# Top-k attention with a mixture-of-depths block: the gate dot products split over GpSimd and ScalarE, all slot picks on VectorE, and the bounds' bits tested once at the end

## The chip, the cores and the metric

The kernel runs on one core of one Trainium2 chip. The metric is the device time of one execution in microseconds (us); a smaller number is better. Five engines run side by side, each through its own instructions in order: TensorE (PE; its weight loads are listed apart as PEld), VectorE (DVE), ScalarE (ACT), GpSimd (POOL) and SyncE (SP), which issues DMAs. An instruction starts when those in front of it on its engine allow it and the semaphores that it waits for have been raised.

## What is computed

For 8 batches and 8 heads, with 576 tokens of 64 dimensions, the reference keeps the 32 largest scores of each query row, takes a softmax over them and multiplies by v. The heads side by side give x (576 tokens x 512). A gate per token is the dot product of x with `w_gate`; the 128 tokens of a batch with the largest gates get an update by a two-layer network:

```python
scores = scale * np.matmul(q, k.transpose(0, 1, 3, 2))
kth = np.partition(scores, -top_k, axis=-1)[..., -top_k:-top_k + 1]
scores = np.where(scores >= kth, scores, -1000000000.0)
...
scores = np.einsum('bsd,d->bs', x, w_gate)
top_idx = np.argpartition(-scores[b], capacity)[:capacity]
ye = np.maximum(x[b, top_idx] @ w1, 0.0) @ w2
g = 1.0 / (1.0 + np.exp(-scores[b, top_idx]))
out[b, top_idx] = x[b, top_idx] + g[:, None] * ye
```

## The kernel before

**Units and steps.** The work is cut into 144 units, 18 per batch: a unit is one block of query rows (t = 0 to 3 with 128 rows each, t = 4 with the last 64) and two heads (four for t = 4). The loop at L1094 walks over steps n; in each step different units stand at different stages, so that a unit takes five steps to pass through. In step n:

- PE: `weigh` (L1036) turns the scores of unit n-4 into `ptr` and `av` in nine pairs of matmuls, and the second of each pair adds the mask `less`; then it turns 0 to 2 loaded pieces of the next batch's q and k, multiplies the scores of unit n+1 (`multiply`, L355), multiplies unit n-4's weights with v (`values`, L503), and runs what the mixture of an earlier batch has due (`h_ps`, `y_ps`, `pick`).
- ACT: two exponentials of unit n-4 out of `ptr` and `av` (outputs `pT` and `last`), half the mask of unit n-3 (`less`), copies of what PE turned (`kT`, `qT`) and of earlier mixture results, the scores of unit n+1 out of PSUM (`sc<-ps`), the values of unit n-4 (`xs<-av`), and two `sides` instructions with a sum for unit n-1. The callbacks in the list `late` run at `flush()` (L1127), behind the mask and in front of the copies.
- POOL: the other half of the mask of unit n-3, then what stands in `vector_late` and `pool_late`, then two multiplications `y<-sc,sides` of unit n-1 and a small `fill`.
- DVE: `find_bound` (L386) for unit n, in two halves with `flush_vector()` between them (L394), then `find_kth` (L437) for unit n-2.

`ptr`, `av` and the score PSUM tile have one buffer each. `keep_in_program_order` fixes every engine's order as it is written; no scheduler changes it.

**The gates.** When the last unit of a block t is through, `normalise` (L543) divides by the sums, one step later: a reciprocal on DVE and the multiplication `x<-xs,rden` on POOL, put at the front of `vector_late`. One step later again `gates` (L954) computes the dot product with `wg` on DVE in one instruction with a sum (`prod<-x,wg`, L940). Counted in steps i = 0 to 17 of a batch, `normalise` stands at i = 2, 4, 8, 12 and 16 and the gate at i = 3, 5, 9, 13 and 17; i = 5 belongs to the block of 64 rows of the batch before.

**The mixture.** `mixture` (L599) is a generator that is advanced at the steps of `mix_at` (L984). The gates go to DRAM and come back as a row on all partitions; per block t, `choose` (L637) counts on DVE how many gates are larger (`junk<-gate_row,gate`, which gives the rank) and `choose_slot` (L656) marks the slot of each rank in `pick` with a comparison: on DVE for t = 0, on POOL for the other four. PE then uses `pick` to place rows, fetched by an indirect DMA from POOL. The last batch goes through `closing` (L746), written out by hand.

**The checks.** `keep_least` (L1073) reduces, once per batch on DVE, the bounds, the values found and the bounds' low mantissa bits (`low`, an integer operation) to one column each of `least`. At the end (L1255 to L1278) nine reductions are folded into `sure`; PE sums it over partitions (`count_unsure`, L1285), and a branch at L1368 runs a general path if a count is off. In PE's order the matmul of `sure` stands behind the four transposes of `xe` of the last batch and in front of that batch's matmuls with w1 and w2.

Of the kernel before, what the change touches and what calls it, by code (L numbers as in the profile page):

```python
# [10 lines left out]
AF = mybir.ActivationFunctionType  # L11
ALU = mybir.AluOpType
FP32 = mybir.dt.float32
BF16 = mybir.dt.bfloat16
I32 = mybir.dt.int32
# [11 lines left out]
LEAST = 1.0e-16 * SMALLER  # L27
# [4 lines left out]
J = 4  # L32
# [16 lines left out]
def kernel(  # L49
# [12 lines left out]
    P = nc.NUM_PARTITIONS  # L62
    B, H, S, D = q.shape
# [5 lines left out]
    R = S - JP  # L69
# [8 lines left out]
    const = ctx.enter_context(tc.tile_pool(name="const", bufs=1))  # L78
# [4 lines left out]
    stats = ctx.enter_context(tc.tile_pool(name="stats", bufs=6))  # L83
    ptpool = ctx.enter_context(tc.tile_pool(name="pt", bufs=2))
    xpool = ctx.enter_context(tc.tile_pool(name="x", bufs=2))
    modpool = ctx.enter_context(tc.tile_pool(name="mod", bufs=1))
# [43 lines left out]

    NS = B * 2 * (J * NHP + NHP // 2)
    seen = const.tile([P, NS], FP32, name="seen")
    least = const.tile([P, 3, B], FP32, name="least")
    sums = const.tile([P, B * NT, H], FP32, name="sums")
    nc.gpsimd.memset(sums, 1.0)

# [27 lines left out]
    wg = const.tile([P, HD], FP32, name="wg")  # L164
# [3 lines left out]
    def load_weights():  # L168
# [6 lines left out]
    pe, dve, act, pool, sp = (  # L175
        InOrder(tc, e)
        for e in (nc.tensor, nc.vector, nc.scalar, nc.gpsimd, nc.sync)
    )


    late, vector_late, pool_late = [], [], []
# [5 lines left out]
    def flush():  # L187
        while late:
            late.pop(0)()
# [353 lines left out]
    def normalise(b, t, xs):  # L543
        n = R if t == J else P
        den = sums[0:n, b * NT + t, :]
        divide(n, xs, of_batch[b][0][0:n, t, :], den)
# [52 lines left out]
    def mixture(row0, pg, rank, exact=False):  # L599
# [8 lines left out]
        if exact:  # L608
            for t0, t1, at in ((0, J, 0), (J, NT, JP)):
                tr = ps_misc.tile([P, 512], FP32, name="tr", tag="misc")  # L610
                n = R if t0 else P
# [6 lines left out]
                w = (t1 - t0) * n  # L618
                act.copy(out=gate_row[:, at : at + w], in_=tr[:, 0:w])
        else:  # L620
            row_dram = drampool.tile([1, S], FP32, name="row_dram")
            sp.dma_start(
                out=row_dram[0, 0:JP].rearrange("(p j) -> p j", j=J), in_=gate[:, 0:J]
            )
            sp.dma_start(
                out=row_dram[0, JP:S].rearrange("(p j) -> p j", j=1),
# [6 lines left out]
        for t in range(NT):  # L633
            yield
            n = R if t == J else P

            def choose(t=t, n=n):  # L637
                junk = modpool.tile([P, S], FP32, name="junk", tag="scratch")
                dve.tensor_scalar(
                    out=junk[0:n, :],  # L640
                    in0=gate_row[0:n, :],
                    scalar1=gate[0:n, t : t + 1],
                    scalar2=None,
                    op0=ALU.is_gt,
                    op1=ALU.add,
                    accum_out=rank[0:n, t : t + 1],
                )
                if exact:
                    break_ties(t, gate, gate_row, rank)

                if t == 0:
                    choose_slot(dve, t, n)
                else:
                    pool_late.append(lambda: choose_slot(pool, t, n))

            def choose_slot(engine, t, n):  # L656
                engine.tensor_scalar(
                    out=pick[0:n, t, :],
                    in0=slot[0:n, :],
                    scalar1=rank[0:n, t : t + 1],  # L660
                    scalar2=None,
                    op0=ALU.is_equal,
                )

            vector_late.append(choose)
# [288 lines left out]
    def gates(b, t):  # L954
        dot_tile(t, *of_batch[b])

    def dot_tile(t, x, pg):
        n = R if t == J else P
        dot(n, x[0:n, t, :], pg[0][0:n, t : t + 1])
# [70 lines left out]
    of_batch = {}  # L1030
# [40 lines left out]
        find_kth(ys.pop(n), next8s[b][:, i, :, :])  # L1071

    def keep_least(b, bound, kth):  # L1073
        low = stats.tile([P, per_batch, 2], I32, name="low", bufs=1)
        dve.tensor_scalar(
            out=low,
            in0=bound.bitcast(I32),
            scalar1=(1 << 23) - 1,
            scalar2=1,
            op0=ALU.bitwise_and,  # L1080
            op1=ALU.bitwise_xor,
        )
        for w, of in enumerate((bound, kth, low)):
            dve.tensor_reduce(
                out=least[:, w, b : b + 1], in_=of, axis=mybir.AxisListType.XY, op=ALU.min
            )

    def mask_of(n, on=None):
        b, i = divmod(n, per_batch)
# [4 lines left out]
    for n in range(-1, N):  # L1094
        b, i = divmod(n, per_batch)
        if i == 0 and 0 <= b < B - 1:
            qkv[b + 1] = room_for_qkv(b + 1)
            loading = chain(
                loading, Rows(k[b + 1], q[b + 1], *qkv[b + 1][0:2]).parts()
            )  # L1100
        if 0 < n + 1 < NHP:
            turn_pair(first_rows, n + 1)
        if n == 1:
            load_v(v[0], qkv[0][2])
        if n == NHP:
            load_weights()


        gating = normalised
        if inverting is not None:  # L1110
            normalised = inverting[0:2]
            vector_late.insert(0, lambda a=inverting: normalise(*a))
            inverting = None
        else:
            normalised = None
        if gating is not None:
            vector_late.append(lambda a=gating: gates(*a))

        if is_unit(n - 4):
            tr, av = room_to_turn()
            pT, last, exp = weigh(scs.pop(n - 4), tr, av, masks.pop(n - 4))
            exp()
        if is_unit(n - 3):
            mask_of(n - 3, (act, None) if n in scatter_steps else None)
        flush()  # L1127
        if is_unit(n + 1):
            b, t, g = units[n + 1]
            ps = room_for_scores()  # L1130
            kT, qT = qkv[b][0:2]
            b, i = divmod(n, per_batch)
            loads = list(islice(loading, first_loads[i] if b == 0 else loads_at[i]))
            halves = [ps[:, a, :, HALF : HALF + P] for a in range(2)]
            for load, half in zip(loads, halves):
                load[0](half)
            multiply(t, g, kT, qT, ps)
            for load, half in zip(loads, halves):
                load[1](half)
            scs[n + 1] = keep(ps, n == -1)  # L1140
        if is_unit(n - 4):
            b4, t4, g4 = units[n - 4]
            values(t4, g4, pT, last, av, qkv[b4][2])
            if n in place_steps:
                values_bank[0] = av
                next(mixtures[place_steps[n]])
            if g4 == 0:
                xs = xpool.tile([P, H, DE], FP32, name="xs")
                if t4 == 0:
                    x = xpool.tile([P, NT, HD], FP32, name="x")  # L1150
                    pg = gates_of[b4 % 2]
                    of_batch[b4] = x, pg
            keep_values(t4, g4, av, xs)
            if g4 == groups(t4) - 1:
                inverting = b4, t4, xs
                n4 = R if t4 == J else P
                keep_sums(n4, xs, sums[0:n4, b4 * NT + t4, :])
            while kept:
                kept.pop(0)()


        if is_unit(n):
            bound_of(n)
        flush_vector()
        flush_pool()
        if is_unit(n - 2):
            kth_of(n - 2)
        while after_kth:
            after_kth.pop(0)()


        if is_unit(n - 1):
            what_is_below(n - 1)

        if gating is not None:
            b, t = gating
            if t == J:
                store(out[b], of_batch[b][0])
                mixtures[b] = mixture(float(b * S), of_batch[b][1], ranks[:, b, :])
        for b in mix_steps.get(n, ()):  # L1180
            next(mixtures[b], None)
        b, i = divmod(n, per_batch)
        if i == v_at and 0 <= b < B - 1:
            load_v(v[b + 1], qkv[b + 1][2])
# [68 lines left out]


    keep_least(B - 1, bounds.pop(B - 1)[:, :, :, 7], next8s.pop(B - 1)[:, :, :, 7])  # L1255
    sure = stats.tile([P, 1], FP32, name="sure")
    dve.memset(sure, 1.0)
    for what, op, than, limit in (
        (least[:, 0, :], ALU.min, ALU.is_gt, LEAST),
        (least[:, 1, :], ALU.min, ALU.is_gt, LEAST),  # L1260
        (least[:, 2, :], ALU.min, ALU.is_gt, 0.5),
        (seen, ALU.max, ALU.is_lt, float(MIDDLE)),
        (seen, ALU.min, ALU.is_gt, float(MIDDLE - 16)),
        (sums.rearrange("p t h -> p (t h)"), ALU.min, ALU.is_gt, FEWEST),
        (sums.rearrange("p t h -> p (t h)"), ALU.max, ALU.is_lt, MOST),
    ):
        far = stats.tile([P, 1], FP32, name="far")
        dve.tensor_reduce(out=far, in_=what, axis=mybir.AxisListType.X, op=op)
        dve.scalar_tensor_tensor(
            out=sure, in0=far, scalar=limit, in1=sure, op0=than, op1=ALU.mult  # L1270
        )
# [133 lines left out]
```

## Time and profile before

| what | value |
|---|---|
| time, median of 3 runs | 825.23 us (824.99 to 825.73) |
| profiled execution | 828.44 us; span of its instructions 826.1 us |
| mean granted TensorE clock | 0.99 |
| DVE busy | 787.2 us, 95% of the span |
| PE busy; weight loads | 777.0 us, 94%; 596.5 us, 72% |
| ACT busy | 730.7 us, 88% |
| POOL busy | 715.4 us, 87% |

The profile is of one execution. "Busy" is time in which an engine ran instructions; overlapping instructions count once, so a group's number of instructions times its mean duration can be more than its busy time. A row of the instruction timeline gives the start, the time taken, engine, line, operation, output<-inputs, shapes and the number of instructions merged; behind it, in brackets, idle time of the engine just before and what ended it. L45 is the line of a helper through which all instructions go, so that they are told apart by their tiles. The distance from one start to the next on a busy engine is what an instruction really costs there, and it is shorter than its duration where the next one starts inside it. The list of waits gives engine, tile, what was waited for, total us, times and the longest.

### The profile page before, as it was taken

Reading aid. Unit: us, or ns where it says so; the run is one execution under the profiler, and the core shown is the slowest. Engines: PE = TensorE matmul, PEld = TensorE weight load, DVE = VectorE, ACT = ScalarE, POOL = GpSimd, SP = SyncE. Lnnn points to the kernel's source line nnn. Section 1 sums busy time; section 2 is a strip of 40 time slices with the busy share of each in tenths; the row PEclk is TensorE's granted clock in tenths of the full one; section 3 lists DMA queues with packets and bytes.
Section 4 is the critical chain, followed back from the end, with each engine's and each line's share of the span. In section 5 each row is a group of like instructions: output and inputs, shape, how many; then the busy total and the mean of one; then the engine's idle time right before and its main releaser. Section 6 shows DMA issues by size and latency. Waiting matters only on the chain. (4 is left out here: it accounts for less than half of the span.)

```text
span 826.1 us, 28252 instructions
## 1 busy us (share of the span) xinstructions
PE 777.0 (94%) x10143; PEld 596.5 (72%) x10143; DVE 787.2 (95%) x4651; ACT 730.7 (88%) x1557; POOL 715.4 (87%) x722
## 2 busy tenths in 40 slices
PE   6888888888999999999999999999999999999976
PEld 5566666666887778877787777877787777767744
DVE  7899999999999999999999999999999999999960
ACT  4799999999999999999999999999999999879831
POOL 3799999999899999999899999999999998899831
PEclk9699999999999999999999999999999999999999
DMA  7931111521141221521223221512215102101021
GB/s 170 283 86 40 28 66 28 105 53 27 60 92 36 53 40 59 112 47 34 79 47 86 53 40 60 104 23 54 40 59 112 28 15 66 23 12 18 2 71 30
DMA packets 122133, 50.38 MB, mean 61 GB/s; under 512 B 116417, under 2 KB 116417, under 8 KB 120961
## 3 DMA queue, kind: packets, MB, share of 16 engines
q1 hardware_dynamic: 118672, 43.91, 22.0%
q0 software_dynamic: 1728, 4.20, 2.8%
q8 instruction: 82, 1.34, 0.8%
q14 instruction: 67, 0.54, 0.3%
q10 hardware_dynamic: 1584, 0.39, 0.2%
HBM read 36.93 MB, written 11.55 MB: 59 GB/s over the span
## 5 line engine op out<-in xcount | busy, mean ns | idle before, releaser
L45 POOL TENSOR_TENSOR y<-sc,sides 128x576 f32<-128x576 f32 x288 | 365.1, 1289 | 57.0 <-ACT sides L45 54.3
L45 DVE MAX8 cand<-sc 128x8 f32<-128x82 f32 (+1 forms) x2016 | 314.0, 228 | 2.7 <-ACT sc L45 2.7
L45 POOL TENSOR_SCALAR less<-sc,next 128x576 bf16<-128x576 f32 x135 | 232.5, 1722 | 12.9 <-DVE next L45 10.0
L45 PE MATMUL ptr<-out_of_reach,less 128*128 128x128 bf16 x1136 | 205.3, 220 | 19.5 <-POOL less L45 19.4
L45 ACT ACTIVATE sides<-sc,bound 128x576 bf16<-128x576 f32 x288 | 223.0, 787 | 0.0
L45 PE MATMUL ptr<-ident,sc 128*128 128x128 f32 x1136 | 217.0, 282 | 0.0
L45 DVE MAX8 next<-y 128x8 f32<-128x584 f32 x288 | 204.4, 751 | 1.7 <-POOL y L45 1.6
L45 PEld LDWEIGHTS av<-v,pT 128*64 128x64 f32 x4544 | 144.1, 137 | 66.9 <-ACT last L45 63.2
L45 PE MATMUL ps<-kT,qT 64*128 64x288 f32 (+1 forms) x1280 | 182.0, 431 | 5.2 <-ACT qT L45 5.2
L45 PEld LDWEIGHTS ptr<-ident,sc 128*128 128x128 f32 x1136 | 161.3, 142 | 29.1 <-issue 17.4
L45 ACT ACTIVATE pT<-ptr 128x1024 f32<-128x1024 f32 x142 | 145.3, 1023 | 33.2 <-PE ptr L45 32.2
L45 PE MATMUL av<-v,pT 128*64 128x65 f32 x4544 | 163.7, 224 | 9.3 <-ACT last L45 8.5
L45 ACT COPY sc<-ps 128x1152 f32<-128x1152 f32 (+1 forms) x144 | 162.2, 1126 | 3.5 <-PE ps L45 3.5
L45 PEld LDWEIGHTS <-less 128*128 128x128 bf16 x1296 | 136.1, 106 | 39.2 <-POOL less L45 25.2
L45 PEld LDWEIGHTS ps<-kT,qT 64*128 64x128 f32 (+1 forms) x1280 | 100.2, 178 | 41.5 <-issue 21.2
L45 ACT ACTIVATE less<-sc,next 128x576 bf16<-128x576 f32 x143 | 111.2, 777 | 12.7 <-DVE next L45 10.8
L45 DVE MATCH_REPLACE8 cand<-best,cand 128x21 f32<-128x21 f32 (+1 forms) x576 | 99.0, 180 | 0.0
L45 DVE MAX8 best<-cand 128x8 f32<-128x21 f32 (+1 forms) x576 | 90.5, 190 | 0.0
L45 PE MATMUL h_ps<-xeT,w 128*128 128x128 f32 x464 | 65.8, 286 | 0.0
L45 PEld LDWEIGHTS h_ps<-xeT,w 128*128 128x128 f32 x464 | 55.8, 191 | 9.2 <-issue 5.8
L45 PE MATMUL y_ps<-w,hT 128*128 128x512 f32 x112 | 60.6, 636 | 0.0
L45 ACT ACTIVATION_READ_ACCUMULATOR sides<-sc,bound 128x1 f32 x288 | 59.9, 208 | 0.0
(133 smaller groups left out, 866.4 us busy)
## 6 DMA issues: line engine op xcount, KB each, us to landing
v<-in_v_dram SPq DMA_DIRECT2D x64, 128.0 KB, 4.2
out_dram<-x SPq DMA_DIRECT2D x8, 1024.0 KB, 3.9
rows<-in_k_dram SPq DMA_DIRECT2D x56, 128.0 KB, 2.9
rows<-in_q_dram SPq DMA_DIRECT2D x56, 128.0 KB, 3.1
w<-in_moe_w_dram SPq DMA_DIRECT2D x2, 2048.0 KB
gate_row<-row_dram SPq DMA_DIRECT2D x7, 288.0 KB, 4.4
w<-in_k_dram SPq DMA_DIRECT2D x8, 128.0 KB, 3.2
last<-in_k_dram SPq DMA_DIRECT2D x8, 128.0 KB, 4.0
```

The source lines that it names most:

```text
L45: return lambda *a, **kw: self._tc.keep_in_program_order(fn(*a, **kw))
```

## The change

The dot product becomes two instructions. Right behind the division, POOL multiplies x by `wg` into `xs` (`weigh_gates`); in the next step ACT copies `xs` onto itself with a sum into the gate (`sum_gates`), from the list `late`. DVE no longer computes the gates of the steps in the loop (38 of the 40 blocks); the last two blocks of the last batch still use the old `gates` on DVE. All five slot picks of a batch go to DVE, each with a sum into an unused column `some` (`accum_out`), one step behind their ranks; in `closing` the picks are as they were. Per batch, the integer operation and two of the three reductions of `keep_least` go; instead ACT copies the 36 bounds of each partition into `bounded`. Behind the loop the last copy is issued by a `flush()`, and then one integer operation on 288 columns and reductions over 288 columns instead of 8 do the tests.

In the built program the order of PE's and of SP's instructions is the same as before.

```diff
-    least = const.tile([P, 3, B], FP32, name="least")
+    least = const.tile([P, B], FP32, name="least")
+    bounded = const.tile([P, NS], FP32, name="bounded")
...
-                if t == 0:
-                    choose_slot(dve, t, n)
-                else:
-                    pool_late.append(lambda: choose_slot(pool, t, n))
-
-            def choose_slot(engine, t, n):
-                engine.tensor_scalar(
+                if t:
+                    choose_slot(t - 1)
+                if t == J:
+                    choose_slot(t)
+
+            def choose_slot(t):
+                n = R if t == J else P
+                some = stats.tile([P, 1], FP32, name="some")
+                dve.tensor_scalar(
                     out=pick[0:n, t, :],
                     in0=slot[0:n, :],
                     scalar1=rank[0:n, t : t + 1],
                     scalar2=None,
                     op0=ALU.is_equal,
+                    op1=ALU.add,
+                    accum_out=some[0:n, :],
                 )
...
+    def weigh_gates(b, t, xs):
+        n = R if t == J else P
+        pool.tensor_tensor(
+            xs[0:n, :, 0:D],
+            of_batch[b][0][0:n, t, :].rearrange("p (h d) -> p h d", h=H),
+            wg[0:n, :].rearrange("p (h d) -> p h d", h=H),
+            ALU.mult,
+        )
+
+    def sum_gates(b, t, xs):
+        n = R if t == J else P
+        act.activation(
+            xs[0:n, :, 0:D],
+            xs[0:n, :, 0:D],
+            AF.Copy,
+            accum_out=of_batch[b][1][0][0:n, t : t + 1],
+        )
...
     def keep_least(b, bound, kth):
-        low = stats.tile([P, per_batch, 2], I32, name="low", bufs=1)
-        dve.tensor_scalar(
-            out=low,
...
-        for w, of in enumerate((bound, kth, low)):
-            dve.tensor_reduce(
-                out=least[:, w, b : b + 1], in_=of, axis=mybir.AxisListType.XY, op=ALU.min
-            )
+        at = 2 * per_batch * b
+        late.append(
+            lambda: act.copy(
+                out=bounded[:, at : at + 2 * per_batch].rearrange("p (n i) -> p n i", i=2),
+                in_=bound,
+            )
+        )
+        dve.tensor_reduce(
+            out=least[:, b : b + 1], in_=kth, axis=mybir.AxisListType.XY, op=ALU.min
+        )
...
-            normalised = inverting[0:2]
-            vector_late.insert(0, lambda a=inverting: normalise(*a))
+            normalised = inverting
+
+            def divide_and_weigh(a=inverting):
+                normalise(*a)
+                weigh_gates(*a)
+
+            vector_late.insert(0, divide_and_weigh)
...
         if gating is not None:
-            vector_late.append(lambda a=gating: gates(*a))
+            late.append(lambda a=gating: sum_gates(*a))
...
     keep_least(B - 1, bounds.pop(B - 1)[:, :, :, 7], next8s.pop(B - 1)[:, :, :, 7])
+    flush()
+    low = modpool.tile([P, S], I32, name="low", tag="scratch")[:, 0:NS]
+    dve.tensor_scalar(
+        out=low,
+        in0=bounded.bitcast(I32),
...
-        (least[:, 0, :], ALU.min, ALU.is_gt, LEAST),
-        (least[:, 1, :], ALU.min, ALU.is_gt, LEAST),
-        (least[:, 2, :], ALU.min, ALU.is_gt, 0.5),
+        (bounded, ALU.min, ALU.is_gt, LEAST),
+        (least, ALU.min, ALU.is_gt, LEAST),
+        (low, ALU.min, ALU.is_gt, 0.5),
```

More of the change, by code (lines that the diff above doesn't have):

```diff
@@ L1073, in keep_least @@
     def keep_least(b, bound, kth):
-        low = stats.tile([P, per_batch, 2], I32, name="low", bufs=1)
-        dve.tensor_scalar(
-            out=low,
[L1077 to L1081, printed above, removed]
-        )
-        for w, of in enumerate((bound, kth, low)):
-            dve.tensor_reduce(
-                out=least[:, w, b : b + 1], in_=of, axis=mybir.AxisListType.XY, op=ALU.min
-            )
+        at = 2 * per_batch * b
[4 more added lines that the diff above has]
+            )
+        )
+        dve.tensor_reduce(
+            out=least[:, b : b + 1], in_=kth, axis=mybir.AxisListType.XY, op=ALU.min
+        )
     def mask_of(n, on=None):
@@ L1175 @@
         if gating is not None:
-            b, t = gating
+            b, t, _ = gating
             if t == J:
@@ L1255 @@
     keep_least(B - 1, bounds.pop(B - 1)[:, :, :, 7], next8s.pop(B - 1)[:, :, :, 7])
+    flush()
[3 more added lines that the diff above has]
+        in0=bounded.bitcast(I32),
+        scalar1=(1 << 23) - 1,
+        scalar2=1,
+        op0=ALU.bitwise_and,
+        op1=ALU.bitwise_xor,
+    )
     sure = stats.tile([P, 1], FP32, name="sure")
```

## The prediction, made before the changed kernel ran

> **What bounds the kernel now.** I read the busy times stage by stage first. The columns are the stretch, its length, then busy time of PE, PEld, DVE, ACT and POOL, the granted clock, DMA share and GB/s; the rows are batch 1, batch 4 and batch 7 (the last).
>
> ```profile
> 102.90:197.90 95.00, 83.34 (x1187) 63.31 (x1188) 94.93 (x563) 88.60 (x190) 88.51 (x88) 1.00 0.25 55
> ...
> 390.30:486.40 96.10, 94.93 (x1263) 73.59 (x1262) 95.99 (x578) 91.51 (x196) 88.52 (x88) 1.00 0.27 60
> ...
> 678.60:778.70 100.10, 96.92 (x1273) 75.82 (x1271) 98.03 (x589) 87.25 (x183) 89.84 (x89) 1.00 0.13 28
> ```
>
> DVE is never idle in batches 1 to 6. In batch 1 it is alone; in batch 4, which is like 2, 3, 5 and 6, PE is as full, and ACT lacks 4.6 us. Being full does not make DVE the bound, so I looked at whom the others wait for, in batches 3 to 5:
>
> ```profile
> ACT pT L45 <- PE ptr L45: 11.9, 33, 0.6
> ...
> POOL less L45 <- DVE next L45: 3.9, 10, 0.6
> ```
>
> ACT's idle time is waiting for PE's turned scores, 4.0 us per batch; waits for DVE are 1.3 us per batch, on POOL. The timeline of ACT's exponentials shows how. Counting from step i = 0 of batch 4:
>
> ```profile
> 395.97 1.03 ACT L45 ACTIVATE pT<-ptr 128x1024 f32<-128x1024 f32 x1
> ...
> 401.23 1.00 ACT L45 ACTIVATE pT<-ptr 128x1024 f32<-128x1024 f32 x1
> ...
> 406.53 1.02 ACT L45 ACTIVATE pT<-ptr 128x1024 f32<-128x1024 f32 x1
> ...
> 422.55 1.02 ACT L45 ACTIVATE pT<-ptr 128x1024 f32<-128x1024 f32 x1 [0.51 <-PE ptr L45]
> ...
> 443.89 1.02 ACT L45 ACTIVATE pT<-ptr 128x1024 f32<-128x1024 f32 x1 [0.51 <-PE ptr L45]
> ```
>
> From 390.67 (i = 0) to 412.07 (i = 4) ACT hardly stops: its own work sets these steps, 5.3 us each. From i = 4 to 17 it waits for PE in nearly each step. There PE has no gap; one step of it:
>
> ```profile
> 426.31 0.27 PE L45 MATMUL ptr<-ident,sc 128*128 128x128 f32 x1
> ...
> 427.85 0.39 PE L45 MATMUL ps<-ident,rows 128*128 128x128 f32 x2
> 428.17 1.24 PE L45 MATMUL ps<-kT,qT 64*128 64x288 f32 x8
> 429.34 1.15 PE L45 MATMUL av<-v,pT 128*64 128x65 f32 x32
> 430.33 0.39 PE L45 MATMUL av<-vpair,last 128*64 128x130 f32 x4
> 430.65 1.16 PE L45 MATMUL h_ps<-xeT,w 128*128 128x128 f32 x8
> 431.64 0.27 PE L45 MATMUL ptr<-ident,sc 128*128 128x128 f32 x1
> ```
>
> From start to start: turning 1.54, loads 0.32, scores 1.17, values 1.31, mixture 0.99, in all 5.33. PE and ACT go in lockstep, for `ptr` has one buffer: the exponentials wait for the turning, the values for the exponentials. `values` comes 1.49 us after the turning, the exponentials need 1.24, so ACT may lag 0.25 us before PE loses time. Taking the longer of PE's and ACT's own work per step, with this slack, I add 21.2 us for i = 0 to 3 (ACT's 5.30, 5.23, 5.27 and 5.40) and 74.7 us for the rest (six steps of PE at 5.33, four at 5.30, then 5.5, 5.5, 5.4 and 5.3, less the lag): 95.9 us of the 96.1. PE and ACT alone explain the batch; DVE is as long, but gives little when it is relieved.
>
> The Trainium skill, "Perfetto Trace Analysis", section "Identifying the Most-Contended Engine", speaks against this reading: the engine of highest occupancy comes first, and TensorE is judged by its weight loads, not its matmuls. By it DVE at 95.99 would bind, PE at 73.59 would have room, and the sum would be the rival "faster" below. I go by the waits, which name PE.
>
> **The change part by part.** All per batch, from the starts of rows.
>
> DVE loses four dot products (rows of 0.67 to 1.1 us) and one of 64 rows, 4.2 us in all from start to start; `low`, 0.97; two reductions, 0.24. It gains five picks with a sum. No such row exists: the same operation `junk` costs 0.28 at 64 columns and 0.79 at 576, so 128 give 0.28 to 0.35; I take 0.29, less the old pick of 0.20: 1.25. Net DVE 96.0 - 4.2 = 91.8.
>
> ACT gains five sums. `sides` with its sum repeats every 0.76 us at 576 columns, `less` without one every 0.67; `sums` on 8 columns costs 0.12. So 512 columns cost 0.61 + 0.09 = 0.70 (between 0.57, what `gy` takes from PSUM, and 0.76). The copy of 36 bounds: 0.15. Sum 3.65: ACT 91.5 + 3.65 = 95.2.
>
> POOL gains five multiplications and loses four picks of 0.61. `x<-xs,rden` on 512 columns takes 1.00, `y<-sc,sides` 1.24 at 576, which is 1.10 at 512; I take 1.05. Net 5.25 - 2.4 = 2.8: POOL 88.5 + 2.8 = 91.3.
>
> No total passes 96.1, so the place decides.
>
> (1) Batches 2 to 6, ACT. The sum stands behind the mask and in front of the copies. At i = 5, 9 and 13 the next exponential idles 0.50 to 0.64 (rows above), 0.70 leaves a lag of 0.2, inside PE's 0.25: nothing. At i = 17 the idle is 0.38, and the next four steps are ACT's own, so 0.32 stays. At i = 3 the idle is 0.02 and the bounds' copy stands one step ahead in the same ACT stretch: 0.68 + 0.13 = 0.81. Together 1.13. Behind the sum queue the scores' copy, for which DVE has over 3 us, and `sides`, for which POOL waits.
>
> (2) Batches 2 to 6, POOL. The multiplication stands between the division and `y`, and delays the next mask, for which PE waits in the middle of its turning. The worst place is i = 4: there `y` starts at 416.82 straight behind the division, and the mask behind it ends 421.20, needed 421.66. With (1), the sum at i = 3 puts `sides` and so `y` of i = 3 about 1.15 later; division and multiplication follow, the mask ends 423.4 (+2.2), while PE is 1.15 later and needs it at 422.8: 0.6 lost. At i = 8 and 12 the masks end 0.90 and 0.56 early, against 1.05 more: 0.15 and up to 0.5, less what a faster DVE gives back (the POOL waits of 0.2 to 0.6 for `next`). Ends 0 and 1.2; I take 0.5.
>
> So 1.6 per batch, in five batches 8.0 us.
>
> (3) Batches 0 and 1. Here DVE binds and PE has room (83.3 of 95.0). In batch 1 DVE falls to 90.7, ACT rises from 88.6 to 92.3 and POOL to 91.3: up to 2.7 could go. But three engines that near to each other, with the added work in lumps, stop one another; I take 1.0 (0 to 2.5). In batch 0 the gates come three times, four steps take 20.2, ACT's part becomes 19.9: 0.5.
>
> (4) Batch 7. Few loads and weaker ACT, but five ranks in three steps on DVE, now with four more picks (+1.2) and fewer dot products; the gate row that DVE waits for 1.86 us comes about 0.8 earlier, for the old dot product ended at 709.1 and the sum should near 708.4. Net -0.3 (-1.5 to +1).
>
> (5) The end. This I hold for the surest part.
>
> ```profile
> 800.93 0.18 DVE L45 TENSOR_SCALAR low<-bound 128x36 int32<-128x36 int32 x1
> ...
> 804.23 0.69 ACT L45 ACTIVATE gy<-y_ps,g 128x512 f32<-128x512 f32 x1 [2.98 <-PE y_ps L45]
> ...
> 804.96 0.16 DVE L45 TENSOR_TENSOR sure<-sure,far 128x1 f32<-128x1 f32 x1
> ...
> 805.41 0.19 PE L45 MATMUL av<-ones,sure 128*1 128x1 f32 x2
> ...
> 806.16 0.49 PE L45 MATMUL ps<-xeT,w 128*128 128x128 f32 x2 [0.56 <-ACT xeT L45]
> ```
>
> The checks run on DVE from 800.93 to 805.12, just in time for PE's matmul of `sure` at 805.41, and behind that matmul queue the last batch's matmuls, 15 us on the path to the end. Afterwards `low` waits for ACT's last copy, which stands behind `gy`, and `gy` starts at 804.23. So `low` starts at 804.23 + 0.57 + 0.24 + 0.05 = 805.09, and all checks behind it. To the end of `sure`: `low` on 288 columns 0.3 (0.1 at 36 columns, 0.42 for `less` on 576), two tests of 288 columns 0.56 each (`seen`), one of 8 columns 0.27, then 2.94 as before (802.18 to 805.12): 4.63, so 809.7. The first matmul with w1 goes from 806.16 to 809.95: +3.8 (3.4 to 4.2). Cover there is none: PE has nothing else in front.
>
> Sum: 8.0 - 1.0 - 0.5 - 0.3 + 3.8 = +10.0. On the profiled execution that is 828.44 to 838.4; it lies 3.2 above the median of the runs, so the forecast is 825.2 + 10.0 = 835.2 us.
>
> **The rivals.**
>
> Faster: DVE binds batches 2 to 6, and PE's gapless rows are stretched waiting. Then each of the five goes to ACT's 95.2 (-0.9), batches 0, 1 and 7 give 1.0, 2.7 and 0.8, the end takes 3.8: 825.2 - 4.5 - 4.5 + 3.8 = 820.0. It decides if PE's own step falls below ACT's 5.29 mean. For it: DVE's zero gaps, PEld's 76%. Against: PE's steps repeat to 0.01 us whatever DVE does beside them, and ACT's waits follow from them. 8%; nearly as large gains that cancel the end, within 0.2% (about what a measurement tells from no change): 5%.
>
> Gates or end hidden: POOL costs nothing and either the end or half of (1) is covered: 828 to 831.5. For the end, ACT would have to run the copy ahead of `gy`; its order says no. 17%.
>
> More: the masks come late at three places per batch (1.2 + 1.13) and batches 0 and 1 gain nothing: 11.7 + 3.8 - 0.3 = +15.2, 840.4. For it: POOL's margins of 0.3 to 0.9 against 1.05. 12%.
>
> Forecast, 831.5 to 838.5: 58%. Range 828.5 to 840.5: it leaves out the 13% at or below no change and a few per cent at each edge. Chances from these cases: slower 0.87, same 0.05, faster 0.08.
>
> **What would show it.** In batches 2 to 6: DVE with 3 us or more of gaps, 97 to 98.3 us per batch, the step from exponential to exponential at i = 3 about 6.1, PE idle on `less` near i = 6; batch 1 at 92.5 to 95. At the end `low` behind `bounded` and the matmul of `sure` near 4 us behind the transposes of `xe`. I am wrong if PE's step falls below 5.3, or if `low` starts before `gy`.

## The result and the profile after

The changed kernel takes 856.03 us (median of 4 runs, 853.28 to 856.47) where the kernel before takes 825.48 on the same chip (824.99 to 825.93, 4 runs). The ratio is 1.0363, with a 95% interval of 1.034 to 1.0386: 30.5 us more, where 10.0 were forecast. The profiled execution took 853.28 us with a span of 851.5; it is the quickest of its runs, while that of before lay 3.2 us above its median. So the spans differ by 25.4 us, and 5 of the 30.5 lie in which executions were profiled. The stages below are read from the two spans.

The first view is the one that the prediction began with: stretch, length, busy time of PE, PEld, DVE, ACT and POOL, granted clock, DMA share, GB/s. The rows are batch 1, batch 4, batch 7 and the end.

```profile
102.30:201.70 99.40, 85.05 (x1177) 64.28 (x1177) 92.25 (x570) 91.35 (x202) 91.32 (x88) 0.97 0.22 53
401.00:500.00 99.00, 95.68 (x1264) 73.42 (x1262) 95.18 (x574) 94.30 (x208) 92.45 (x89) 1.00 0.25 58
697.80:798.70 100.90, 96.95 (x1272) 75.65 (x1271) 95.75 (x573) 89.89 (x193) 93.58 (x90) 1.00 0.12 27
798.70:851.50 52.80, 37.90 (x329) 26.49 (x327) 18.86 (x62) 13.53 (x33) 14.83 (x19) 0.93 0.14 40
```

DVE, which had no gap, now idles 7.2 us in batch 1 and 3.8 in batch 4, and both batches are longer. No engine is full any more: every engine has more idle time in batch 4 than PE and DVE had before, so somebody waits for somebody. All stages follow. A batch runs from where ACT comes free for the exponentials of its step i = 0 to the same point of the next batch; batch 0 begins with the first exponential of all:

| stage | before | after | difference | forecast |
|---|---|---|---|---|
| start | 31.1 | 29.8 | -1.3 | 0 |
| batch 0 | 71.8 | 72.5 | +0.7 | -0.5 |
| batch 1 | 95.0 | 99.4 | +4.4 | -1.0 |
| batch 2 | 96.2 | 100.4 | +4.2 | +1.6 |
| batches 3 to 6 | 384.5 | 395.7 | +11.2 | +6.4 |
| batch 7 | 100.1 | 100.9 | +0.8 | -0.3 |
| end | 47.4 | 52.8 | +5.4 | +3.8 |

The start is not touched by the change; it lies between 29.1 and 31.1 in all profiles of this case, so a difference of 1 us there, or in batch 0 that follows it, says nothing.

The list of waits for batches 3 to 5 (engine, tile, what was waited for, total us, times, longest) names them:

```profile
ACT pT L45 <- PE ptr L45: 12.5, 37, 0.6
...
DVE next L45 <- POOL y L45: 11.1, 15, 1.4
...
PE ptr L45 <- POOL less L45: 7.8, 18, 0.7
```

The first row is nearly as before. The two others are new, and both name POOL: DVE's search `next` waits five times a batch for `y`, PE six times a batch for POOL's half of the mask. POOL's own waits for `next` are gone. The timeline of POOL in batch 1 shows what delays `y`:

```profile
118.83 1.05 POOL L45 TENSOR_TENSOR x<-xs,rden 128x512 f32<-128x512 f32 x1
119.96 1.27 POOL L45 TENSOR_TENSOR xs<-x,wg 128x512 f32<-128x512 f32 x1
121.19 2.53 POOL L45 TENSOR_TENSOR y<-sc,sides 128x576 f32<-128x576 f32 x2
123.67 0.22 POOL L45 TENSOR_TENSOR y<-steps,seen 128x16 f32<-128x16 f32 x1
123.86 1.73 POOL L45 TENSOR_SCALAR less<-sc,next 128x576 bf16<-128x576 f32 x1
```

and DVE's timeline what comes of it:

```profile
123.92 0.77 DVE L45 MAX8 next<-y 128x8 f32<-128x584 f32 x1 [1.89 <-POOL y L45]
```

From start to start the multiplication takes 121.19 - 119.96 = 1.23 us, all of it in front of `y`, and DVE stands still for 1.89. POOL's next mask starts right behind the fill, at 123.86 and so before `next` has run: it waits for nothing but POOL's own queue, where the multiplication now stands in front of it. PE, which needs this mask, stops in the middle of its turning. Two rows of PE's timeline, from batch 4 and from the first steps of batch 1:

```profile
422.60 0.23 PE L45 MATMUL ptr<-out_of_reach,less 128*128 128x128 bf16 x1 [0.58 <-POOL less L45]
```

```profile
102.83 0.23 PE L45 MATMUL ptr<-out_of_reach,less 128*128 128x128 bf16 x1 [2.17 <-POOL less L45]
```

The pause of 2.17 us costs more than its length. The granted clock (third number from the right) behind it, and behind the pause of 4.36 us at the end that is shown further below:

```profile
104.00:106.00 2.00, 2.00 (x9) 1.19 (x8) 2.00 (x19) 1.46 (x3) 2.00 (x4) 0.50 0.16 37
106.00:108.00 2.00, 2.00 (x39) 1.48 (x38) 1.39 (x3) 1.39 (x2) 1.12 (x1) 0.75 0.46 103
```

```profile
829.80:833.50 3.70, 3.70 (x19) 3.67 (x20) 0.22 (x2) 0.00 (x0) 0.00 (x0) 0.50 0.02 3
833.50:835.50 2.00, 2.00 (x17) 2.00 (x17) 0.00 (x0) 0.38 (x1) 0.00 (x0) 0.87 0.00 0
```

Not every pause of this length does so. In the changed kernel's first three batches PE waits eight times for 2.0 to 2.2 us for a mask. Behind three of these waits (ending at 102.83, 136.74 and 202.07) the clock is 0.50 for 3.4 us; behind the other five (59.94, 81.06, 125.65, 159.20 and 180.34) it stays at 1.00.

The end itself goes as the prediction put it:

```profile
824.18 0.69 ACT L45 ACTIVATE gy<-y_ps,g 128x512 f32<-128x512 f32 x1 [2.98 <-PE y_ps L45]
...
824.77 0.25 ACT L45 COPY bounded<-bound 128x36 f32<-128x36 f32 x1
825.05 0.31 DVE L45 TENSOR_SCALAR low<-bounded 128x288 int32<-128x288 int32 x1 [3.96 <-ACT bounded L45]
...
829.44 0.16 DVE L45 TENSOR_TENSOR sure<-sure,far 128x1 f32<-128x1 f32 x1
...
829.75 0.19 PE L45 MATMUL av<-ones,sure 128*1 128x1 f32 x2 [4.36 <-DVE g L45]
...
829.87 3.78 PE L45 MATMUL ps<-xeT,w 128*128 128x128 f32 x16
```

`low` stands behind `bounded`, `bounded` behind `gy`, and the first matmul with w1 starts 5.11 us behind the turning of `xe` (824.76) where it was 1.30 before: +3.81. What the prediction did not have is the last row: these 16 matmuls take 3.78 us, because they run at half clock (0.50 in the row above); before they took 2.05.

### The profile page after: what moved, and what is told of

It reads as the page before. It is cut to its first block, busy times and chain, and to the rows that moved or that the text cites. A ratio compares the mean times of both kernels' runs of the same rounds, so it can differ in the third digit from the quotient of the medians.

```text
span 851.5 us, 28206 instructions
## 1 busy us (share of the span) xinstructions
PE 783.0 (92%) x10143; PEld 597.1 (70%) x10143; DVE 771.2 (91%) x4615; ACT 751.3 (88%) x1641; POOL 744.1 (87%) x732
## 5 line engine op out<-in xcount | busy, mean ns | idle before, releaser
L45 DVE MAX8 cand<-sc 128x8 f32<-128x82 f32 (+1 forms) x2016 | 310.5, 227 | 1.8 <-ACT sc L45 1.8
L45 POOL TENSOR_SCALAR less<-sc,next 128x576 bf16<-128x576 f32 x135 | 235.3, 1743 | 1.1 <-PE av L45 1.1
L45 PEld LDWEIGHTS <-less 128*128 128x128 bf16 x1296 | 134.2, 105 | 61.5 <-POOL less L45 48.2
```

The lines of the kernel that those rows point to most:

```text
L45: return lambda *a, **kw: self._tc.keep_in_program_order(fn(*a, **kw))
```

## The experiments

**Theory T**: POOL's multiplication in front of `y` makes most of the loss. It delays what stands behind it on POOL: `y`, for which DVE's `next` waits, and the next mask, for which PE waits at six places of a batch; some of PE's pauses of 2 us halve the clock for 3.4 us; the end adds its own 5.4. (The expectations below put the mask behind DVE's search. By the rows above it is late through POOL's own queue.) **R1**: ACT's sums make it, by lengthening the lockstep of PE and ACT. **R2**: DVE's part makes it, the picks or a mask on DVE that became slow (further below). **R3**: DVE bound the batches before, and its relief is worth something.

### The three parts one by one

e1: the gates alone, on the kernel before; picks and checks as they were.

> Kernel before, with the gates alone moved: GpSimd multiplies behind its division, ScalarE sums; slot picks and checks stay as they were. Theory T (the multiplication of 1.24 us stands in front of y on GpSimd, so VectorE's search and then the mask come late for TensorE, at six places of a batch; two pauses over 2 us also halve TensorE's clock for some us): most of the loss is here, +18 to +26 us on before, batches 3 to 6 at 98 to 99.5 us each and batch 1 at 97 to 100. Rival R1 (ScalarE's five sums lengthen the lockstep of ScalarE and TensorE, GpSimd is covered): +4 to +7 us, that is 5 batches of 0.8 to 1.3. Rival R3 (VectorE bound before and the relief is worth something): batches 0 and 1 shorter than before by 1 us or more.

e2: the picks alone (the diff's part on `choose_slot`).

> Kernel before, with the slot picks alone changed: all five on VectorE with a sum, none on GpSimd. VectorE has no gap in batches 1 to 6 and gets four picks more and the sums, some 1.25 us per batch. T: VectorE has become the longest by 1.25 in batch 1 and nearly that in 2 to 6, GpSimd's relief of 2.4 us gives nothing: +3 to +8 us. A rival, R2 (the picks make most of the changed kernel's loss by pushing VectorE's search back): +15 us or more. If GpSimd's relief is what matters, the kernel is faster than before.

e3: the checks alone (`least`, `bounded`, `keep_least` and the end).

> Kernel before, with the checks alone changed: ScalarE copies the bounds, their bits are looked at once at the end. T: the end grows by 5.4 us as in the changed kernel (3.8 by the late checks, 1.6 by the lower clock behind TensorE's pause of 4.4 us); VectorE loses 1.2 us per batch, which gives back up to 1.2 in batches 0 and 1 and little in 2 to 6: +2.5 to +5 us in all. If VectorE binds the batches (R3), each of seven gives back near 1.2: -3 us or faster than before.

| kernel | ratio to before, 95% interval | batch 1 | batch 2 | batches 3 to 6, each | batch 7 | end |
|---|---|---|---|---|---|---|
| before | 1 | 95.0 | 96.2 | 96.1 to 96.2 | 100.1 | 47.4 |
| changed | 1.0363, 1.034 to 1.0386 | 99.4 | 100.4 | 98.8 to 99.0 | 100.9 | 52.8 |
| e1, gates | 1.0277, 1.0235 to 1.032 | 98.6 | 100.6 | 98.8 to 99.0 | 101.1 | 47.2 |
| e2, picks | 1.0061, 1.0042 to 1.008 | 96.3 | 96.6 | 96.9 | 101.5 | 47.2 |
| e3, checks | 1.0047, 1.0031 to 1.0064 | 94.5 | 96.6 | 95.9 to 96.2 | 99.0 | 53.3 |

The excesses add up to 2.77 + 0.61 + 0.47 = 3.85%, against 3.63% for all three together. The gates alone make the batches of the changed kernel to 0.2 us in 2 to 6; the checks alone make its end. R2's picks cost 0.8 us a batch when DVE is not relieved. All three as T expected, and R3 gets nothing: batch 1 grows with the gates.

### Multiplication or sum

e4: the changed kernel without the multiplication (the gate becomes the plain sum of the row as it is ahead of the division).

```diff
                 normalise(*a)
-                weigh_gates(*a)
```

> The changed kernel without GpSimd's multiplication: ScalarE sums the row as it stands, so the multiplication by the gate's weights is left out and the gate is the plain sum of the row. T: the delay of y is gone, batches 0 to 6 fall back to what ScalarE's sums alone cost, batches 3 to 6 at 96 to 97.3, batch 1 at 91 to 95, the end stays at +5.4: +3 to +9 us on before in place of +30. R1 (the sums): nearly all stays, +22 or more.

e5: the changed kernel with a sum over one column.

```diff
-            xs[0:n, :, 0:D],
-            xs[0:n, :, 0:D],
+            xs[0:n, 0:1, 0:1],
+            xs[0:n, 0:1, 0:1],
             AF.Copy,
```

> The changed kernel with ScalarE's sum over one column in place of 512: it leaves out all but one of 512 terms of each gate, GpSimd's multiplication stays. T (the multiplication in front of y makes the loss): the sums cost next to nothing because ScalarE's queue was waiting for TensorE anyway, +24 to +30 us on before. R1 (the sums lengthen the lockstep of ScalarE and TensorE): at most +10 us is left of +30.

Without the multiplication the ratio is 1.0058 (1.0029 to 1.0087); without the sums it is 1.0331 (1.0314 to 1.0348), hardly less than with them. The stages of e4, batch 1 and batch 4, in the columns of before:

```profile
100.90:192.90 92.00, 82.70 (x1181) 62.54 (x1179) 89.54 (x561) 90.81 (x202) 85.23 (x83) 1.00 0.25 57
387.10:483.70 96.60, 94.82 (x1264) 73.37 (x1261) 93.05 (x573) 93.62 (x209) 86.17 (x84) 1.00 0.27 60
```

Batch 1 is at 92.0: 3.0 less than before, and 7.4 less than with the multiplication. DVE's waits for `y` in batch 1 fall from 5.9 to 2.4 us, and the clock is back at 1.00. Batch 4 is at 96.6, so 2.4 of its 2.9 us were the multiplication's. Batches 3 to 6 of e5 stay at 98.7 to 98.8. R1 falls: the sums cost nothing as long as PE is late for another reason. Batch 1 of e5 takes 101.0, longer than the changed kernel's 99.4; the clock fell behind four of its pauses there (ending at 103.81, 126.64, 159.08 and 181.61), against two in the changed kernel.

### DVE's relief by itself

e6: the kernel before, with the dot product in the loop over 64 of 512 columns.

```diff
+            in0=x[0:n, t, 0:D],
+            in1=wg[0:n, 0:D],
...
-            vector_late.append(lambda a=gating: gates(*a))
+            vector_late.append(lambda a=gating: short_dot(*a))
```

> Kernel before with VectorE's gate dot product over 64 of 512 columns in the batches' loop: it leaves out seven eighths of the product, and frees VectorE of about 3.5 us per batch with no work put elsewhere. Lockstep of ScalarE and TensorE (batches 2 to 6 not bound by VectorE): 0 to 0.6 us per batch there, and 2 to 3 us in each of batches 0 and 1: -4 to -8 us. VectorE bound: 2.5 us or more in each of batches 2 to 6 too: -15 us or more.

The ratio is 0.9944 (0.9928 to 0.9959). Batches 2 to 6 are at 95.9 to 96.0, so 0.2 to 0.3 less each; batch 1 is at 93.0, batch 0 at 70.5 (2.0 and 1.3 less, where 2 to 3 were expected), batch 7 at 98.5. The relief of DVE, with nothing put elsewhere, is worth what the lockstep reading gave it: little in batches 2 to 6, where DVE was full. R3 falls, and with it any hope that moving this work could bring more than 5 us.

### The end

e7: e3 with the last copy of bounds in front of `gy` on ACT.

```diff
     sums_of(J, xs)
+    keep_least(B - 1, bounds.pop(B - 1)[:, :, :, 7], next8s.pop(B - 1)[:, :, :, 7])
+    flush()
     next(closed)
...
-    keep_least(B - 1, bounds.pop(B - 1)[:, :, :, 7], next8s.pop(B - 1)[:, :, :, 7])
-    flush()
     low = modpool.tile([P, S], I32, name="low", tag="scratch")[:, 0:NS]
```

> Kernel before with the new checks alone, but the last batch's copy of its bounds put in front of gy on ScalarE. If the wait of the checks for that copy makes the loss at the end, the end falls from 53.3 to 47 to 48.5 us and the kernel is as fast as before or up to 4 us faster. If the longer tests on VectorE make it, the end stays above 50 us.

e8: the changed kernel, PE kept busy while it waits for `sure`.

```diff
+        for _ in range(64):
+            pe.matmul(ps[:, P : 2 * P], out_of_reach, out_of_reach)
         pe.matmul(ps[0:1, 0:1], sure, ones)
```

> The changed kernel with 64 needless matmuls of 128x128 in bf16 on TensorE in front of the matmul that waits for the checks. If the pause of 4.4 us lowers the granted clock and so lengthens the last stage, the 16 matmuls with w1 take 2.1 us in place of 3.8 and the end falls from 52.8 to 51 to 51.5. If the clock has another cause, the end stays at 52.8 or grows by the time of the added matmuls.

In e7 the end takes 47.2 us, as before the change, and the whole 0.999 of before (0.9979 to 1.0002): the copy's place behind `gy` was the whole loss of the end. In e8 it takes 50.9, in PE's timeline:

```profile
827.93 3.74 PE L45 MATMUL av<-out_of_reach 128*128 128x128 bf16 x64
832.39 0.19 PE L45 MATMUL av<-ones,sure 128*1 128x1 f32 x2 [0.72 <-DVE ones L45]
832.51 2.05 PE L45 MATMUL ps<-xeT,w 128*128 128x128 f32 x16
```

With 3.74 us of needless work in the pause the first 16 matmuls take 2.05 us again and not 3.78. The end is 1.9 us shorter for it. So of the end's 5.4 us some 1.6 to 1.9 are the clock's and the rest, 3.5 to 3.8, is waiting.

### Size and place of the multiplication

e9: half of its columns (the other half stays unweighed).

```diff
-            xs[0:n, :, 0:D],
+            xs[0:n, 0 : H // 2, 0:D],
...
```

> The changed kernel with GpSimd multiplying 256 of 512 columns: half of each multiplication is left out. T: y and the mask come 0.62 us late instead of 1.24; the masks had 0.3 to 0.9 us to spare, so more than half of the loss goes: batches 3 to 6 at 96.8 to 98, batch 1 at 93 to 97, +10 to +18 us on before. If every microsecond on GpSimd counted alike, batches 3 to 6 would be at 97.8 and the whole at +18.

e10: the whole multiplication behind `y` and `fill`, and so in front of POOL's next mask.

```diff
-                weigh_gates(*a)
...
             what_is_below(n - 1)
+        if normalised is not None:
+            weigh_gates(*normalised)
```

> The changed kernel with the multiplication behind y in GpSimd's queue instead of in front of it. T: VectorE's search no longer waits 1.9 us for y at each gate step of batches 0 and 1 (the waits of next for y fall from 39 to under 25 us); but GpSimd's next mask now stands behind the multiplication, so TensorE still waits: batches 3 to 6 at 97.5 to 99, +14 to +25 us on before. If the place does not matter (GpSimd is simply too full): as the changed kernel within 2 us, in batches 0 and 1 too. If the time GpSimd waits there for VectorE covers it: +10 us or less.

e9: ratio 1.0143 (1.012 to 1.0166), batches 3 to 6 at 96.9, batch 1 at 93.9. Half the multiplication, 0.73 us in the rows, costs 0.3 in each of batches 3 to 6 over e4's 96.6, the other half 2.0. That is a threshold and no rate: in batch 4 only one step of e9 is longer than in e4 (i = 5, 5.59 against 5.33), so at the other places the first half costs nothing.

e10 was worse than T had it: ratio 1.0751 (1.0729 to 1.0773), 103.5 us in batches 3 to 6. The masks' part is no larger (PE's waits for `less` fall from 37.0 to 33.6 us in the whole run), and DVE's waits for `y` do fall, to 22.1. The loss is a new wait, in which T had not looked. The list of waits, then ACT's timeline:

```profile
ACT xs L45 <- POOL xs L45: 58.0, 37, 2.3
```

```profile
436.22 0.63 ACT L45 ACTIVATE xs<-xs 128x512 f32<-128x512 f32 x1 [1.50 <-POOL xs L45]
```

The sum stands at its place in ACT's order, in front of the copies of scores and values. The multiplication behind `y` ends later than ACT gets there, by 1.6 us on average in 37 gates, and ACT's whole queue, scores included, waits with the sum. In the changed kernel the multiplication in front of `y` was done in time for it.

### A mask that became slow

In each of six batches one mask is made on DVE, and in five of them it became slow (the sixth, at 762.66, took 0.62 us). Their group between 300 and 700 us (busy time, mean ns of one, idle time before them) had a mean of 505 ns before the change; after it, it is

```profile
L45 DVE TENSOR_SCALAR less<-sc,next 128x576 bf16<-128x576 f32 x5 | 17.0, 3398 | 0.0
```

e11 gives this mask a sum that nobody uses.

```diff
+                            op1=ALU.add,
+                            accum_out=some,
```

> The changed kernel with a sum added to the mask that VectorE makes in five of the batches, which took 3.4 us beside GpSimd's multiplications and 0.5 us in the kernel before. If the form of the instruction is what lets GpSimd hold it up, it takes 0.6 to 1.0 us now. T: no more than 2 us of the whole comes back, since TensorE waits for GpSimd's masks, not for this one. R2 (the stalled mask makes the loss of batches 2 to 6): 5 us or more come back, 1 us in each.

```profile
L45 DVE TENSOR_SCALAR_CACHE_REDUCE less<-sc,next 128x576 bf16<-128x576 f32 x4 | 3.2, 798 | 0.0
```

The mask takes 0.80 us instead of 3.40, and the kernel is not faster for it: ratio 1.0368 (1.0346 to 1.0389). R2 falls. DVE had 3.8 us to spare in a batch.

### Could the gates be placed without loss?

e12: three of five gates, each multiplied in two halves, one and two steps behind the division; the sum a step later; the rest as before.

```diff
+            if normalised[1] < J - 1:
+                weigh_in[n + 1] = *inverting, 0
+                weigh_in[n + 2] = *inverting, 1
+                sum_in[n + 3] = inverting
```

> Kernel before, with the gates of three of five token tiles moved, GpSimd's multiplication in two halves of 0.62 us, one and two steps behind its division and not beside it, the sum on ScalarE a step later; two gates, the picks and the checks stay as they were. T: the lateness per step stays within what the masks have to spare; batches 3 to 6 at 95.7 to 96.6, batches 0 and 1 shorter by 1 to 2 us each because VectorE is relieved: -1 to -5 us on before. If whatever GpSimd does in front of y comes back in full on TensorE: three of five gates cost +8 us or more.

e13: e12 with sums over one column. e14: as e12, but the whole multiplication at n + 1 and the sum at n + 2.

> e12_split3 with ScalarE's sums over one column: all but one of 512 terms of three gates per batch are left out. If the 0.9 us that batches 3 to 6 still lost there are the sums' own time, at the steps in which ScalarE has no idle time, they come back to 96.0 to 96.4. If GpSimd's multiplications still make them, even in halves, they stay at 96.8 or more.

> Three of five gates moved as in e12_split3, but the whole multiplication of 1.24 us one step behind the division, and the sum two steps behind it, in the steps in which ScalarE waits 0.5 us for TensorE. If place decides for both (GpSimd in a step without a division, ScalarE where it is idle), batches 3 to 6 come to 96.1 to 96.6, and the whole is -3 to +2 us on before. If an uncut multiplication costs in any step, 97 or more.

e15: e14 with the checks of e7.

> e14_later3 with the new checks and the last copy of bounds in front of gy as in e7_checks_early. Batches 0, 1 and 7 gain by VectorE's relief (2 to 4 us in all), 2 to 6 nothing, the end nothing: -2 to -6 us on before, if e14 does not lose in batches 2 to 6; otherwise as before or slower.

| kernel | ratio to before, 95% interval | batch 1 | batch 2 | batches 3 to 6, each | end |
|---|---|---|---|---|---|
| e12 | 1.0084, 1.0064 to 1.0105 | 94.3 | 99.5 | 97.0 to 97.1 | 47.7 |
| e13 | 1.0013, 1.0004 to 1.0023 | 93.6 | 98.8 | 96.5 to 96.6 | 47.6 |
| e14 | 1.0073, 1.0058 to 1.0089 | 94.0 | 99.4 | 96.8 to 96.9 | 47.6 |
| e15 | 1.0081, 1.0067 to 1.0095 | 93.3 | 98.7 | 97.0 to 97.4 | 47.7 |

T expected e12 faster and e14 level, and missed; for e15 its expectation left both open, and with e14's loss the slower case came. A smaller lump in a free step lowers the price per gate (0.3 us against the changed kernel's 0.6 in batches 3 to 6: 0.9 for three, 2.8 for five), but not to nothing. Of e12's 0.9 us about half go with the sums: e13 lands between its two expectations. In e14, from i = 10 to 12 and from 13 to 16 the steps add up to those of before within 0.15 us: there the gates are hidden. The 0.7 us arise at i = 0 to 3. At i = 0 the step takes 5.88 us in place of 5.30, and the sum stands behind the mixture's `gy` in an ACT stretch without idle time:

```profile
393.92 0.69 ACT L45 ACTIVATE gy<-y_ps,g 128x512 f32<-128x512 f32 x1
394.49 0.64 ACT L45 ACTIVATE xs<-xs 128x512 f32<-128x512 f32 x1
```

At i = 1 the step is 0.3 longer, and PE waits 0.77 us for POOL's mask; i = 3 gives 0.2 back. e13 loses 0.7 us at i = 1 although its sums are over one column, so there it is not the sum.

Batch 2 loses 2.5 to 3.3 us in all four: near i = 1 PE waits 1.9 us (e12 and e13) or 2.5 us (e14 and e15) for POOL's mask. Behind it the clock is 0.50 for 3.4 us in e12, e13 and e14, as in the changed kernel; in e15 it stays at 1.00, and batch 2 loses 2.5 us all the same. In this place a gate's multiplication meets the fetching of `xe` on POOL while DVE is still late from batch 1; that this coincidence is the reason is argued from the order of the rows, and no run took it apart. No version that keeps the whole computation beats the kernel before beyond its interval.

## Why the prediction was wrong

**Direction and place** were right: PE and ACT set batches 2 to 6 in lockstep, DVE's full row there gives little when relieved (e6), and place, not totals, decides. The rival "faster" fell with e6, "gates or end hidden" with e1 and e3. "More" named the right mechanism, late masks and no gain in batches 0 and 1, and was still 15 us short. Two of the signs came: the step at i = 3 took 5.96 us in batch 4, and PE waited for `less` at i = 6 (0.50 us, at 433.93). What failed are the terms (2) and (3), and (5) in part.

**Step (2), POOL in batches 2 to 6, is the term that was too small**: 0.5 us a batch, bounds 0 and 1.2; the multiplication cost 2.4 in batch 4 (changed 99.0 against e4's 96.6) and by the same comparison 2.9 in batch 2. The multiplication was put at 1.05 and takes 1.24, but that is the lesser part. The prediction asked at three of the five divisions (i = 4, 8, 12) whether one mask comes late and took the faster DVE off. The trace shows six waits per batch, two steps behind each division (i = 4, 6, 10, 14 and 0, and i = 2, where the mask came at the last moment before too), of 0.23 to 0.58 us in batch 4. The first mask behind a multiplication on POOL is the one that PE uses two steps behind the division, and it had 0.3 to 0.9 us to spare against 1.24 more in front of it. The lateness does not last: `y`, fill and mask take 4.36 us from start to start on POOL (411.42 to 415.78 in batch 4) where a step lasts 5.3, and the mask behind a late one is early again (done at 427.16, used at 427.95). Against e4, batch 4 loses 0.67, 0.41 and 0.53 us behind the three divisions that were asked about, 0.48 behind the one at i = 16, and 0.2 elsewhere; the faster DVE gave nothing back, for POOL no longer waited for `next`.

**Step (3), batches 0 and 1, has the wrong sign**: -1.5 against +5.1 measured. The relief was there and larger than the upper bound (e4: -3.0 in batch 1), but the prediction's list of what is queued behind the multiplication named the masks and forgot DVE's `next`, which waits for `y`. Where DVE is the bound, its waits go into the time: 5.9 us in batch 1, 3.5 more than in e4; another 1.0 is waiting for scores. The rest of the 7.4 us there was not separated further; PE's long pauses, two of them with a drop of the clock, fall into the same batch.

**Step (1), ACT's sums**: 0.70 forecast, 0.52 + 0.09 = 0.61 from start to start. The 1.13 us a batch that it added up to are not seen in the changed kernel, for PE was late for the masks anyway (e5); with the multiplication gone all that is left of sums, picks and copies is 0.5 (e4). Steps i = 9 and 13 hid their sums, as forecast; the idle time fails to hide the sum in e14 where `gy` stands in the same stretch.

**Step (4)**, batch 7, gave +0.8 against -0.3, inside its bounds of -1.5 and +1. **Step (5)**, the end, was right in the wait (3.81 against 3.8), and 1.6 us short, because it priced a pause of PE at its length: behind the pause 16 matmuls took 3.78 us in place of 2.05.

In sum: forecast +10.0; in the spans +25.4, of which batches 2 to 6 are 15.4 against 8.0, batches 0 and 1 5.1 against -1.5, the end 5.4 against 3.8, batch 7 0.8 against -0.3, and the start -1.3.

## What to carry to other kernels

When work is put into an engine's queue in front of something that others wait for, list every consumer behind it on all engines, and hold the lump against the time to spare of each of them: here 1.24 us against 0.3 to 0.9, at every one of five places. Idle time in an engine's total is no room, and the second half of a piece of work can cost many times the first (2.0 against 0.3 us here). A check moved to the end is free only if nothing in front of it on its engine waits for something late.

## What the runs showed of the hardware

A pause of PE can cost more than its length. Behind the pause of 4.3 to 4.4 us at the end the granted clock was 0.50 in all seven kernels that have it, and 64 needless matmuls in this pause gave 1.9 us of the end back. Behind pauses of 1.9 to 2.5 us it fell sometimes: in the changed kernel behind three of eight, each time to 0.50 for 3.4 us. A pause of 2.47 us at the same place of batch 2 was followed by a drop in e14 (at 202.17) and by none in e15 (at 202.20); no run shows what decides. The Trainium skill, "TensorE: Matmul & The Clock Gate", section "Part 1: The HAM clock gate", says the clock halves after an idle window of some 3.4 us that runs freely; the drops behind waits of about 2 us here show that a shorter pause can do.

A plain comparison on DVE, SBUF to SBUF, took 3.40 us beside POOL's back-to-back instructions and 0.50 before the change, when it began while POOL was idle; with a sum it took 0.80 beside them. In batch 4 it started at 401.26, inside a DMA issue of POOL (400.71 to 401.79) and 0.56 us ahead of two multiplications of 1.24, and ended 0.3 us behind the second one. The Trainium skill, "SBUF — State Buffer", section "SBUF: two separate sides", tells of a port pair that DVE's two-port instructions and GpSimd lock against each other for a whole instruction; the rows agree, and show besides that DVE got no turn between one instruction of GpSimd and the next.
